# First eight heads reordered, early casts on ScalarE, and a shorter general path in an attention, expert and gated-layer kernel

## The chip, the cores and the metric

The kernel runs on one core of one Trainium2 chip. The metric is device microseconds of one execution, the median of the runs.

## The reference

```python
def _attn_ref(q, k, v, g_q, g_k):          # q, k, v: (4, 12, 448, 64)
    q_n, k_n = rmsnorm(q, g_q), rmsnorm(k, g_k)
    scores = 1 / sqrt(64) * q_n @ k_n.T
    attn = exp(scores - max(scores)); attn /= sum(attn) + 1e-9
    return attn @ v

def _moe_ref(x, expert_emb, tau, w1, w2):  # x: (1792, 768), 8 experts, hidden 1024
    logits = (x / |x|) @ (expert_emb / |expert_emb|).T / tau
    e = argmax(logits); g = softmax(logits)[e]
    return g * (relu(x @ w1[e]) @ w2[e])

def _moe2_ref(x, w_gate, w_val, w_out):    # hidden 1536
    return (sigmoid(x @ w_gate) * (x @ w_val)) @ w_out
```

All is float32. The three run one after the other on the same 1792 rows.

## The kernel before

The program has three stages. `attention` goes over 48 heads (4 batches of 12). The 448 rows of a head lie on 112 partitions, 4 rows (r = 0 to 3) on each. Two heads form a group g; two or four heads are loaded as a unit u. `experts` sorts the rows by expert into a table in HBM and multiplies each expert's window of rows with its weights. `glu` is the gated layer. TensorE (PE) multiplies in pairs of float32r products: each operand is cast into a high part, and the rest, a low part, is subtracted.

The path of a head n in `attention`: `squares` and `stats` make the reciprocal root mean squares of q and k (for unit 0 a chain of ten small steps on VectorE, `rsqrt`; for later units two on ACT and five on GpSimd, `pool_rsqrt`). `scale_k` scales k; `scale_q` scales q, but for group 0, whose q is not scaled: there the scale goes into the maxima and the exponentials. `high_q` and `low_q` make the parts of q, `high_v` and `low_v` those of v. `turn_k` and `turn_q` transpose on PE; `high_k`, `low_k` and `copy_q` bring the results to SBUF, with the gain vector `gsc`. Then for each r: `scores` (two matmuls of PE), `peaks` (VectorE takes the negated maximum, L326; for the two heads of group 0 it multiplies it with the scale, L328), `exps` (ACT, L337), `turn_p` (four transposes), `high_p`, `low_p`, `values`. `copy_o`, `outputs` and `weigh` finish the head.

The scores have two PSUM buffers (`pss`), so the scores of a row block wait for the exponential two before it. `squares` runs on ACT for the first part of groups 0 to 3, on GpSimd later; group 0's k is squared by VectorE. `copy` takes an engine number: 0 is ACT, 1 VectorE, 3 GpSimd; `early(g)` is true for groups 1 to 7.

The order is written out by hand. Every call is put into a list by `at(place, f, ...)`; `chain` puts the steps of a generator one after the other, and `steps_of` takes some steps at one place. Places count row blocks, four to a head; `PLACE` holds those of the steady state, `EARLY` and `EARLY_LOADS` those of groups 1 to 7, and numbers below zero the time before head 0. The list is sorted by place, and each engine runs its instructions in that order. The DMA loads of q, k and v go on SP's queue, one unit after the other (`load`, L176), and so do the two gain vectors (`gains_load`, L598) between unit 0's q and v.

At the end of attention `plan` (on VectorE) works out from the experts' counts where each window lies, and `most`, how far the fullest expert exceeds its window. Meanwhile PE multiplies the first rows of the first expert (`soon_hidden`, taken in steps of two matmuls by `steps_of` at four places; L851). `load_most` (L862) brings `most` into a register of every engine, and `experts` starts with a branch (L1138): only where `most` is above zero is `beyond` run, a general path for experts with more rows than their window. With these inputs it is jumped over. PE goes on with L855.

```python
        with tc.If(soon["most"] > 0):
            beyond(pools)
```

Of the kernel before, what the change touches and what calls it, by code (L numbers as in the profile page):

```python
# [21 lines left out]
def tile_attention_moe_glu(  # L22
# [29 lines left out]
    MORE = min(WIN)  # L52
# [74 lines left out]
    EARLY_LOADS = [-19.988, -7.521, -2.583, 3.821, 11.99]  # L127
    EARLY = [
# [9 lines left out]
    def attention(ctx2, rp, after):  # L138
# [30 lines left out]
        def load(u):  # L169
# [3 lines left out]
            for src, dst in ((k, qk[:, 1]), (q, qk[:, 0]), (v, vv)):  # L173
# [455 lines left out]
        for g in range(NGT):  # L629
# [1161 lines left out]
```

## Time and profile before

| | |
|---|---|
| runs (three), us | 1183.16, 1183.21, 1185.81; median 1183.21 |
| profiled execution, us | 1183.76 |
| its span on the core, us | 1182.1 |
| PE busy | 1139.1 us (96%) |
| PE weight loads busy | 1053.4 us (89%) |
| VectorE busy | 867.3 us (73%) |
| ScalarE busy | 574.3 us (49%) |
| GpSimd busy | 319.1 us (27%) |
| DMA | 154.54 MB, 131 GB/s |

The span is what the profile covers; the execution's own time is 1.66 us longer. Busy shares are averages over stages of very different kind, so they are read by stretch.

### The profile page before, as it was taken

What the parts mean: (1) busy time and instruction counts of PE and PEld (TensorE: products, weight loads), DVE (VectorE), ACT (ScalarE), POOL (GpSimd) and SP (SyncE); (2) the same over time, 40 slices, a digit from 0 to 9 for tenths busy, and PEclk for the clock granted to TensorE, in tenths of its full rate; (3) what the DMA queues carried; (4) which work ended last, traced back from release to release, by engine and by line L of the source; (5) the groups of instructions that cost most, each with busy time, mean ns of one, the idle gap of its engine ahead of it and who ended that gap; (6) DMA issues with size and microseconds to landing.
All of it is one profiled execution on the core that took longest, in us unless ns stands there. A gap on an engine that the chain in (4) does not pass through costs nothing.

```text
span 1182.1 us, 19579 instructions
## 1 busy us (share of the span) xinstructions
PE 1139.1 (96%) x7198; PEld 1053.4 (89%) x7199; DVE 867.3 (73%) x1650; ACT 574.3 (49%) x1285; POOL 319.1 (27%) x484
## 2 busy tenths in 40 slices
PE   4899999999999999999999999999999999999996
PEld 3688888787888999999999999999999999999996
DVE  7999898898884145566677887887888878346673
ACT  5788988998993143556665521221212121332220
POOL 5765778779752000000000000010000000021132
PEclk9999999999999999999999999999999999999998
DMA  5414823111063164666676233443444343932031
GB/s 120 111 37 114 254 56 95 47 48 49 27 206 113 55 209 139 206 194 212 213 221 189 89 111 130 147 160 112 151 139 134 120 142 99 352 119 98 21 134 53
DMA packets 97942, 154.54 MB, mean 131 GB/s; under 512 B 4891, under 2 KB 82459, under 8 KB 96947
## 3 DMA queue, kind: packets, MB, share of 16 engines
q1 hardware_dynamic: 91379, 125.70, 34.8%
q0 software_dynamic: 6432, 27.53, 6.2%
q8 instruction: 58, 0.95, 0.3%
q14 instruction: 41, 0.34, 0.1%
q10 hardware_dynamic: 32, 0.02, 0.0%
HBM read 117.84 MB, written 35.39 MB: 130 GB/s over the span
## 4 chain that ended last, share of the span: by engine, by line
PE 62%; issue 3%; POOL 1%; DMA 1%; POOLq 0%
PE psg L1125 42%; PE pso L1125 8%; PE psg L1129 5%; PE psg L855 2%; PE psg L1132 2%; POOL out_dram L754 1%; PE psg L851 1%; PE psw L1160 1%; DMA wout<-wod 1%; PE psw L822 0%; POOL dummy L761 0%; PE pso L1103 0%; POOLq L1787 0%; POOLq L754 0%
## 5 line engine op out<-in xcount | busy, mean ns | idle before, releaser
L1125 PE MATMUL psg<-xs,w 128*128 128x448 f32 x1728 | 351.3, 365 | 0.0
L1125 PEld LDWEIGHTS psg<-xs,w 128*128 128x128 f32 x1728 | 323.9, 188 | 27.1
L1435 POOL DMA_DIRECT2D wod<-so x42 | 22.9, 544 | 604.2 <-DVE hA L1577 349.9
L1125 PE MATMUL pso<-wout,hs 128*128 128x384 f32 x882 | 153.4, 335 | 0.4 <-DMA wout<-wod 0.4
L1125 PEld LDWEIGHTS pso<-wout,hs 128*128 128x128 f32 x882 | 152.9, 188 | 0.7 <-issue 0.7
L978 DVE TENSOR_TENSOR whl<-raw,whl 128x768 fp32r<-128x768 f32 (+1 forms) x98 | 105.1, 1073 | 60.1 <-ACT whl L974 59.9
L337 ACT ACTIVATE pn<-pss,nm 112x448 f32<-112x448 f32 x184 | 119.7, 651 | 28.2 <-DVE nm L326 26.5
L326 DVE TENSOR_REDUCE nm<-pss 112x1 f32<-112x448 f32 x192 | 118.4, 617 | 8.9 <-PE pss L319 8.6
L374 DVE TENSOR_TENSOR pl<-pst,ph 112x448 fp32r<-112x448 f32 x180 | 110.6, 614 | 17.3 <-ACT ph L361 16.0
L354 PEld LDWEIGHTS pst<-ident,pn 112*112 112x112 f32 x768 | 88.0, 134 | 25.6 <-DVE pl L374 5.7
L354 PE MATMUL pst<-ident,pn 112*112 112x112 f32 x768 | 106.3, 260 | 4.5 <-DVE pl L374 4.4
L361 ACT CAST ph<-pst 112x448 fp32r<-112x448 f32 x180 | 97.3, 541 | 11.0 <-PE pst L354 8.1
L388 PE MATMUL psv<-ph,vt 112*128 112x448 f32 x204 | 91.8, 460 | 0.0
L319 PE MATMUL pss<-kh,qt 128*112 128x448 f32 x192 | 79.3, 413 | 12.8 <-ACT pn L337 11.7
L974 ACT CAST whl<-raw 128x768 fp32r<-128x768 f32 (+1 forms) x98 | 90.7, 926 | 0.0
L1413 ACT CAST w<-cva 128x384 fp32r<-128x384 f32 x48 | 24.7, 515 | 109.2 <-DVE cva L1397 104.2
L1125 PE MATMUL psg<-hhl,whl 128*128 128x288 f32 (+3 forms) x576 | 75.1, 287 | 0.0
L319 PE MATMUL pss<-kl,qt 128*112 128x448 f32 x192 | 71.8, 374 | 0.0
L1125 PEld LDWEIGHTS psg<-hhl,whl 128*128 128x128 f32 x576 | 70.9, 189 | 0.1
L1125 PE MATMUL psg<-xhl,whl 128*128 128x288 f32 (+3 forms) x576 | 70.0, 283 | 0.0
L1125 PEld LDWEIGHTS psg<-xhl,whl 128*128 128x128 f32 x576 | 69.4, 188 | 0.0
L388 PE MATMUL psv<-pl,vt 112*128 112x448 f32 x180 | 65.6, 365 | 0.0
(287 smaller groups left out, 2003.6 us busy)
## 6 DMA issues: line engine op xcount, KB each, us to landing
raw<-in_moe_w_dram SPq DMA_DIRECT2D x28, 768.0 KB, 4.5
raw<-in_moe_w_dram SPq DMA_DIRECT2D x21, 1024.0 KB, 5.4
wod<-so POOLq DMA_DIRECT2D x42, 384.0 KB, 2.6
wout<-wod SPq DMA_DIRECT2D x7, 2304.0 KB, 9.6
raw<-in_moe_w_gate_dram SPq DMA_DIRECT2D x24, 384.0 KB, 3.3
raw<-in_moe_w_val_dram SPq DMA_DIRECT2D x24, 384.0 KB, 3.2
raw<-in_moe_w_out_dram SPq DMA_DIRECT2D x24, 384.0 KB, 3.1
xs<-zero SPq DMA_DIRECT2D x8, 960.0 KB, 7.2
```

The lines of the kernel that those rows point to most:

```text
L319: nc.tensor.matmul(ps[:P, :S], lhsT=qt[:, r * P : (r + 1) * P], rhs=kk, start=(i == 0), stop=(i == 1))
L326: nc.vector.tensor_reduce(out=nm, in_=sc[n, r][:P, :S], axis=AX.X, op=ALU.max, negate=True)
L337: nc.scalar.activation(out=pn[n][:, r], in_=sc.pop((n, r))[:P, :S], func=AF.Exp, bias=sc.pop((n, r, "m")), scale=scale(0, 0, n, 1)[:, r] i ...
L354: nc.tensor.transpose(ps[:P, r * P : (r + 1) * P], p[:, r, c * P : (c + 1) * P], ident[:P, :P])
L361: nc.scalar.copy(out=ph, in_=pt[n, c][0][:P, :S])
L374: nc.vector.tensor_tensor(out=pl, in0=ps[:P, :S], in1=ph.bitcast(F32), op=ALU.subtract)
L388: nc.tensor.matmul(ps[:, :S], lhsT=lhs, rhs=p, start=(c == 0 and i == 0), stop=(c == R - 1 and i == len(parts) - 1),)
L974: nc.scalar.copy(out=splits[p][:, 0, cs], in_=raws[p][:, cs])
L978: nc.vector.tensor_tensor(out=w[:, 1, cs], in0=raws[p][:, cs], in1=w.bitcast(F32)[:, 0, cs], op=ALU.subtract)
L1125: nc.tensor.matmul(ps, lhsT=lhs[:, a], rhs=rhs[:, b], start=first and i == 0, stop=last and i == 2)
L1129: nc.tensor.matmul(ps.rearrange("p (a n) -> p a n", n=n), lhsT=lhs[:, 0], rhs=rhs, start=first, stop=False)
L1413: nc.scalar.copy(out=hi, in_=af)
```

## The change

What it does:

- `load` brings q ahead of k in every unit; unit 1's load is moved up behind unit 0's; the gain vectors are loaded from ACT's queue.
- In group 0 the casts and differences of q come first, and ACT squares k too, after the cast of q. The squares of groups 1 to 3 are put at places of their own.
- `scale_k`, `turn_k`, `high_k` and `low_k` of head 1 move behind the first scores of head 0. Head 2's steps stand at places of their own (`SECOND`).
- The first maxima (heads 0 and 1) are multiplied with the scale by ACT, ahead of the exponential, in place of VectorE; the product has a tile of its own.
- For groups 1 to 7 the casts `high_q` and `high_v` go from VectorE to ACT.
- `constants` (GpSimd) and the experts' norm come later.
- `soon_hidden` takes 29 steps in place of 25 ahead of the load of `most`.
- `beyond` is written with windows of 128 rows in place of 192 and loops over the weights' columns.

```diff
-    MORE = min(WIN)
+    MORE = 128
...
-        sum_squares=17.264, choice=16.838, norms=22.659, ranks=26.111, gate_x=45.151, second=9.104,
-        constants=7.485, emb_norm=1.692, emb_step=0.342, emb_turn=10.124, guard=-0.094, first_v=-13.224,
+        sum_squares=17.264, choice=16.838, norms=22.659, ranks=26.111, gate_x=45.151, 
+        constants=20.3, emb_norm=3.5, emb_step=0.342, emb_turn=13.3, guard=-0.094, first_v=-13.224,
     )
+    SECOND = (5.0, 5.35, 5.585, 5.9, 6.25)
...
-    EARLY_LOADS = [-19.988, -7.521, -2.583, 3.821, 11.99]
+    EARLY_LOADS = [-19.988, -19.987, -2.583, 3.821, 11.99]
     EARLY = [
-        [-12.0, 0.85, 1.0, 0.9, 2.342, 0.398, 2.863, 1.588],
...
+        [-19.8705, 1.43, 1.51, 1.5, 3.45, 6.6, 3.47, 7.0],
...
-            for src, dst in ((k, qk[:, 1]), (q, qk[:, 0]), (v, vv)):
+            for src, dst in ((q, qk[:, 0]), (k, qk[:, 1]), (v, vv)):
...
-            if i == 0 and (g < 4 or ENG_SQ[g % NG]):
+            if g == 0 or i == 0 and (g < 4 or ENG_SQ[g % NG]):
                 nc.scalar.activation(out=sq[:, sl], in_=x, func=AF.Square)
...
-            copy(0 if g == 0 else 1 if early(g) else ENG_QS[g % NG], qs[:, :, 0], heads(nat[unit_of[g][0]][0][:, 0], g))
+            copy(0 if g <= 7 else 1 if early(g) else ENG_QS[g % NG], qs[:, :, 0], heads(nat[unit_of[g][0]][0][:, 0], g))
...
-            copy(0 if g == 0 else 1 if early(g) else ENG_VT[g % NG], vt[:, :, D : 2 * D], heads(nat[unit_of[g][0]][1], g))
+            copy(0 if g <= 7 else 1 if early(g) else ENG_VT[g % NG], vt[:, :, D : 2 * D], heads(nat[unit_of[g][0]][1], g))
...
             if n < G:
-                nc.vector.tensor_tensor(out=nm, in0=nm, in1=scale(0, 0, n, 1)[:, r], op=ALU.mult)
+                raw, nm = nm, sm.tile([P, 1], F32, tag="nms", name="nms", bufs=4)
+                sc[n, r, "raw"] = raw
...
+            if n < G:
+                nc.scalar.activation(
+                    out=sc[n, r, "m"], in_=sc.pop((n, r, "raw")), func=AF.Copy, scale=scale(0, 0, n, 1)[:, r]
+                )
...
-                nc.sync.dma_start(out=t, in_=src.unsqueeze(0).to_broadcast([2, D]))
+                nc.scalar.dma_start(out=t, in_=src.unsqueeze(0).to_broadcast([2, D]))
...
-                for place, n in ((-0.4, 2), (0.16, 9), (0.17, 25), (1.2, 99)):
+                for place, n in ((-0.4, 2), (0.16, 9), (0.17, 29), (1.2, 99)):
...
-                halves(w1, NC, xt, F // 2, to_hidden)
-                halves(w2, nfc, ht, DM // 2, to_rows)
+                for w, kc, x, y, func in ((w1, NC, xt, ht, AF.Relu), (w2, nfc, ht, yt, AF.Copy)):
+                    to = y.rearrange("p f n -> p (f n)")
+                    with tc.For_i(0, w.shape[2], 128) as col:
+                        wa = ov.tile([128, nfc, 128], F32, tag="ow", name="ow")
+                        part = w[bass.ds(ex, 1), :, bass.ds(col, 128)]
+                        nc.sync.dma_start(out=wa[:, 0:kc], in_=part.rearrange("o (c p) f -> p (o c) f", p=128))
+                        ps = gemm_ps()[:, :MORE]
+                        for c in range(kc):
+                            nc.tensor.matmul(ps, lhsT=wa[:, c], rhs=x[:, c], start=(c == 0), stop=(c == kc - 1))
+                        nc.scalar.activation(out=to[:, bass.ds(col, MORE)], in_=ps, func=func)
```

In these rows sq, qs, qt, kh, kl, vt, nm, nms are the tiles of the steps named above, st those of the reciprocal roots; a number behind a name is its buffer. The beginning of ACT's program, before:

```order
L191 ACTIVATE sq_143<-qk_121 112x512
L267 CAST qs_145<-qk_121 112x8x64
L267 CAST qt_153<-psq_148 128x448
L287 ACTIVATE kh_171<-psk_165,gsc_71 128x448
L267 CAST qt_178<-psq_173 128x448
L287 ACTIVATE kh_185<-psk_180,gsc_71 128x448
L267 CAST vt0_116<-vv_122 112x8x64
L191 ACTIVATE sq_207<-qk_135 112x1024
```

and now:

```order
L604 DMA gsc_71<-in_g_q_dram 128x1x1
L604 DMA gk_125<-in_g_k_dram 128x1x1
L268 CAST qs_129<-qk_121 112x8x64
L192 ACTIVATE sq_135<-qk_121 112x512
L192 ACTIVATE sq_138<-qk_121 112x512
L268 CAST qt_158<-psq_153 128x448
L192 ACTIVATE sq_163<-qk_140 112x1024
L288 ACTIVATE kh_180<-psk_174,gsc_71 128x448
L268 CAST qt_187<-psq_182 128x448
L268 CAST vt0_116<-vv_122 112x8x64
```

The gain vectors' loads stand first, the cast of q ahead of both squares, and a square of unit 1 (112x1024) ahead of the first `high_k`. The second `high_k` is gone from here. PE at the same place, before:

```order
L301 MATMUL psq_148<-ident_70,qs_145 128x112 x4
L281 MATMUL psk_165<-ident_70,ks_162 128x112 x4
L301 MATMUL psq_173<-ident_70,qs_145 128x112 x4
L281 MATMUL psk_180<-ident_70,ks_162 128x112 x4
L319 MATMUL pss_229<-kh_171,qt_153 112x448
L319 MATMUL pss_229<-kl_191,qt_153 112x448
L319 MATMUL pss_240<-kh_171,qt_153 112x448
L319 MATMUL pss_240<-kl_191,qt_153 112x448
```

and now:

```order
L302 MATMUL psq_153<-ident_70,qs_129 128x112 x4
L282 MATMUL psk_174<-ident_70,ks_172 128x112 x4
L302 MATMUL psq_182<-ident_70,qs_129 128x112 x4
L320 MATMUL pss_218<-kh_180,qt_158 112x448
L320 MATMUL pss_218<-kl_200,qt_158 112x448
L320 MATMUL pss_229<-kh_180,qt_158 112x448
L320 MATMUL pss_229<-kl_200,qt_158 112x448
L282 MATMUL psk_238<-ident_70,ks_172 128x112 x4
```

The transposes of head 1's k (the second psk) stand behind the first two pairs of scores. VectorE, up to its first maximum (nm), before:

```order
L73 TENSOR_SCALAR st0_129<-st1_130 112x8
L292 SCALAR_TENSOR_TENSOR kl_191<-psk_165,gsc_71,kh_171 128x448
L78 TENSOR_TENSOR st1_130<-st0_129 112x8
L80 TENSOR_TENSOR st1_130<-st1_130,st2_131 112x8
L82 SCALAR_TENSOR_TENSOR st1_130<-st1_130 112x8
L84 SCALAR_TENSOR_TENSOR st0_129<-st1_130,st0_129 112x8
L86 TENSOR_TENSOR st1_130<-st0_129 112x8
L88 SCALAR_TENSOR_TENSOR st1_130<-st1_130,st2_131 112x8
L292 SCALAR_TENSOR_TENSOR kl_199<-psk_180,gsc_71,kh_185 128x448
L90 SCALAR_TENSOR_TENSOR st0_129<-st1_130,st0_129 112x8
L326 TENSOR_REDUCE nm_232<-pss_229 112x1
L328 TENSOR_TENSOR nm_232<-nm_232,st0_129 112x1
```

and now:

```order
L73 TENSOR_SCALAR st0_132<-st1_133 112x8
L78 TENSOR_TENSOR st1_133<-st0_132 112x8
L293 SCALAR_TENSOR_TENSOR kl_200<-psk_174,gsc_71,kh_180 128x448
L80 TENSOR_TENSOR st1_133<-st1_133,st2_134 112x8
L82 SCALAR_TENSOR_TENSOR st1_133<-st1_133 112x8
L84 SCALAR_TENSOR_TENSOR st0_132<-st1_133,st0_132 112x8
L86 TENSOR_TENSOR st1_133<-st0_132 112x8
L88 SCALAR_TENSOR_TENSOR st1_133<-st1_133,st2_134 112x8
L90 SCALAR_TENSOR_TENSOR st0_132<-st1_133,st0_132 112x8
L327 TENSOR_REDUCE nm_222<-pss_218 112x1
L327 TENSOR_REDUCE nm_232<-pss_229 112x1
L234 TENSOR_TENSOR ks_172<-qk_121,st0_132 112x512
```

The second `low_k` (kl) and the product L328 are gone, and half of the scaling of k (ks) comes behind two maxima. PE at the branch around `beyond`, before (oxw, oxt, oht and ow are the tiles of `beyond`):

```order
L1138 COMPARE_AND_BRANCH
L1325 COMPARE_AND_BRANCH
L1325 UNCONDITIONAL_BRANCH x2
L1787 BRANCH_PREFETCH_HINT
L1326 ISA
L1326 TENSOR_LOAD tabs
L1326 COMPARE_AND_BRANCH
L1336 MATMUL psg<-ident,oxw 128x96 x12
L1350 MATMUL psg<-oxt,ow 128x192 x48
L1350 MATMUL psg<-oht,ow 128x192 x48
```

and now:

```order
L1150 COMPARE_AND_BRANCH
L1336 COMPARE_AND_BRANCH
L1336 UNCONDITIONAL_BRANCH x2
L1784 BRANCH_PREFETCH_HINT
L1337 ISA
L1337 TENSOR_LOAD tabs
L1337 COMPARE_AND_BRANCH
L1348 MATMUL psg<-ident,oxw 128x128 x6
L1352 COMPARE_AND_BRANCH
L1352 UNCONDITIONAL_BRANCH x2
L1784 BRANCH_PREFETCH_HINT
L1358 MATMUL psg<-oxt,ow 128x128 x6
```

Between the branch and the end of `beyond` there were 12, 48 and 48 matmuls; there are 6 and 6 here and 8 in a second loop behind these rows.

## Rows read from the trace of the kernel before

**Rows 1.** windows: us, busy us (instructions) by engine, PE to POOL; clock, DMA

```profile
15.94:33.95 18.01, 12.26 (x55) 9.03 (x56) 15.89 (x30) 12.44 (x32) 14.51 (x38) 1.00 0.38 90
33.95:50.00 16.05, 13.40 (x97) 10.65 (x95) 15.86 (x29) 11.67 (x32) 9.44 (x14) 1.00 0.37 88
50.00:80.00 30.00, 28.83 (x201) 24.03 (x202) 27.69 (x52) 25.83 (x69) 21.59 (x26) 1.00 0.20 47
80.00:116.00 36.00, 35.26 (x252) 29.35 (x251) 34.18 (x67) 30.81 (x82) 18.65 (x19) 1.00 0.44 120
```

**Rows 2.** timeline, first 16 us: start, us, engine, line, operation, tiles [idle before]

```profile
4.04 0.69 DVE L193 TENSOR_TENSOR sq<-qk 112x512 f32<-112x512 f32 x1 [3.92 <-DMA qk<-in_k_dram]
...
4.57 0.63 ACT L191 ACTIVATE sq<-qk 112x512 f32<-112x512 f32 x1 [2.44 <-DMA qk<-in_q_dram]
...
5.10 0.60 ACT L267 CAST qs<-qk 112x512 fp32r<-112x512 f32 x1
...
5.70 0.17 DVE L69 TENSOR_SCALAR st<-st 112x8 int32<-112x8 int32 x1
5.78 1.26 POOL L251 TENSOR_TENSOR qs<-qk,qs 112x512 fp32r<-112x512 f32 x1 [2.48 <-ACT qs L267]
5.90 1.16 DVE L73 TENSOR_SCALAR st<-st 112x8 int32<-112x8 int32 x1
...
8.50 1.29 DVE L233 TENSOR_TENSOR ks<-qk,st 112x512 f32<-112x512 f32 x2
...
11.63 1.01 PE L281 MATMUL psk<-ident,ks 112*128 112x112 f32 x4 [0.62 <-ACT qt L267]
...
13.94 1.24 DVE L90 SCALAR_TENSOR_TENSOR st<-st,st 112x8 f32<-112x8 f32 x1
...
15.94 0.72 ACT L337 ACTIVATE pn<-pss,nm,st 112x448 f32<-112x448 f32 x1 [0.23 <-DVE nm L328]
```

**Rows 3.** DMA view, 2 to 8 us: busy tenths and GB/s in 40 slices

```profile
DMA  9437999999752000099499999000000000003799
GB/s 150 109 109 273 355 328 396 362 348 205 171 116 48 0 0 0 0 41 75 41 130 151 89 68 21 0 0 0 0 0 0 0 0 1 0 21 137 253 328 328
```

**Rows 4.** timeline: a cast and a one-element operation on ACT

```profile
13.20 0.61 ACT L267 CAST vt<-vv 112x512 fp32r<-112x512 f32 x1
...
24.61 0.18 ACT L96 ACTIVATE en<-en 8x1 f32<-8x1 f32 x1
```

**Rows 5.** lines view, DVE, 0 to 34 us: count, busy us, mean ns

```profile
L328 DVE TENSOR_TENSOR nm<-nm,st 112x1 f32<-112x1 f32 x8 | 3.4, 430 | 0.3
```

**Rows 6.** windows view of line L271 alone: us, DVE busy us (instructions)

```profile
33.95:116.00 82.05, 7.77 (x11) 1.00 0.34 87
```

**Rows 7.** timeline, 366 to 391 us, PE around the branch

```profile
366.89 7.04 PE L851 MATMUL psg<-soon_x,soon_w 128*128 128x160 f32 x50
...
374.38 3.50 PE L851 MATMUL psg<-soon_x,soon_w 128*128 128x160 f32 x24 [0.45 <-issue]
...
380.17 10.61 PE L855 MATMUL psg<-soon_hh,soon_w 128*128 128x160 f32 x64 [2.29 <-PEq L1138]
```

**Rows 8.** line L1138 by sequencer: ns min, median, max; start us

```profile
L1138 DVEq COMPARE_BRANCH  x1: 72/72/72, 374.4 to 374.4; - x1
...
L1138 PEldq COMPARE_BRANCH  x1: 4406/4406/4406, 375.3 to 375.3; - x1
L1138 POOLq COMPARE_BRANCH  x1: 45/45/45, 376.0 to 376.0; - x1
```

**Rows 9.** view of line L862: the register load on PE

```profile
L862 PEldq TENSOR_LOAD <-most x1: 1178/1178/1178, 373.1 to 373.1; - x1
```

**Rows 10.** windows view, 380 to 388 us, columns as in rows 1

```profile
380.20:382.00 1.80, 1.80 (x9) 1.80 (x10) 0.00 (x0) 0.00 (x0) 0.25 (x2) 0.64 0.31 57
382.00:384.00 2.00, 2.00 (x9) 2.00 (x9) 0.00 (x0) 0.00 (x0) 0.00 (x0) 0.50 0.77 229
...
386.00:388.00 2.00, 2.00 (x17) 2.00 (x16) 0.00 (x0) 0.00 (x0) 0.00 (x0) 1.00 0.32 119
```

More of the change, by code (lines that the diff above doesn't have):

```diff
@@ L636, in attention @@
             if g:
-                chain(ts, 0.2 if g > 1 else 0.8, squares(g, later=14))
+                if g < 4:
+                    work = squares(g)
+                    for place in (ts, *((0.925, 0.93), (2.95, 2.96), (9.4, 9.6))[g - 1]):
+                        at(place, steps_of, work, 1)
+                else:
+                    chain(ts, 0.2, squares(g, later=14))
                 if j == 0:
@@ L645, in attention @@
         at(start, load, 0)
-        chain(start, 0.001, squares(0, 1, 1))
-        chain(start + 0.125, 0, squares(0, 0, 1), 1, start + 0.21)
+        at(start + 0.001, high_q, 0)
+        at(start + 0.002, low_q, 0)
+        chain(start + 0.003, 0.001, squares(0, 1, 1))
+        chain(start + 0.005, 0, squares(0, 0, 1), 1, start + 0.21)
         chain(start + 0.1, 0.01, stats(0, 1, 1))
@@ L651, in attention @@
         for place, f, *a in (
-            (0.126, high_q, 0), (0.127, low_q, 0), (0.202, scale_k, 0, 0, 1), (0.203, scale_k, 0, 1, 1),
-            (0.128, turn_q, 0), (0.129, copy_q, 0), (0.206, turn_q, 1), (0.207, copy_q, 1),
-            (0.204, turn_k, 0), (0.205, high_k, 0), (0.2225, low_k, 0),
-            (0.208, turn_k, 1), (0.209, high_k, 1), (0.2285, low_k, 1),
+            (0.128, turn_q, 0), (0.129, copy_q, 0), (0.202, scale_k, 0, 0, 1),
+            (0.204, turn_k, 0), (0.205, high_k, 0), (0.206, turn_q, 1), (0.207, copy_q, 1), (0.2235, low_k, 0),
         ):
             at(start + place, f, *a)
-        at(PLACE["first_v"], high_v, 0)
-        at(PLACE["first_v"], low_v, 0)
+        at(-19.7908, high_v, 0)
+        at(-0.09, low_v, 0)
+        for place, f, *a in ((0.922, scale_k, 0, 1, 1), (0.93, turn_k, 1), (1.42, high_k, 1), (1.95, low_k, 1)):
+            at(place, f, *a)
         for n in range(N):
-            lead = {0: -8.5, G: PLACE["second"]}.get(n, n * R)
-            for f in (turn_k, high_k, low_k, turn_q, copy_q) if n >= G else ():
-                at(lead + PLACE[f.__name__], f, n)
+            for i, f in enumerate((turn_k, high_k, low_k, turn_q, copy_q) if n >= G else ()):
+                at(SECOND[i] if n == G else n * R + PLACE[f.__name__], f, n)
             for r in range(R):
@@ L1296, in beyond @@
     def beyond(pools):
[L1298 removed]
+        K = -(-(NT - min(WIN)) // MORE)
         N = E * K
[L1300 removed]
         ov = tc.alloc_tile_pool(name="ov", bufs=1, side="left")
@@ L1340, in beyond @@
-                ht = ov.tile([128, nfc, MORE], F32, tag="oht", name="oht")
-                def halves(w, kc, x, width, evict):
-                    for h in range(2):
-                        wa = ov.tile([128, kc, width], F32, tag="ow", name="ow")
-                        part = w[bass.ds(ex, 1), :, h * width : (h + 1) * width]
-                        nc.sync.dma_start(out=wa, in_=part.rearrange("o (c p) f -> p (o c) f", p=128))
-                        for f in range(width // 128):
-                            ps = gemm_ps()
-                            for c in range(kc):
-                                nc.tensor.matmul(
-                                    ps[:, :MORE], lhsT=wa[:, c, f * 128 : (f + 1) * 128], rhs=x[:, c],
-                                    start=(c == 0), stop=(c == kc - 1),
-                                )
-                            evict(h * width // 128 + f, ps[:, :MORE])
@@ L1356, in to_hidden @@
-                def to_hidden(f, ps):
-                    nc.scalar.activation(out=ht[:, f], in_=ps, func=AF.Relu)
-                def to_rows(o, ps):
-                    nc.scalar.copy(out=x2[:, o, bass.ds(dst, MORE)], in_=ps)
-                halves(w1, NC, xt, F // 2, to_hidden)
-                halves(w2, nfc, ht, DM // 2, to_rows)
+                xw = ov.tile([MORE, DM], F32, name="oxw")
+                nc.sync.dma_start(out=xw, in_=xs[bass.ds(src, MORE)])
+                xt, ht, yt = [ov.tile([128, n, MORE], F32, name=name) for name, n in (("oxt", NC), ("oht", nfc), ("oyt", NC))]
@@ new lines, in beyond @@
+                for c0 in range(0, NC, 4):
+                    n = min(4, NC - c0)
+                    ps = gemm_ps()[:, : n * MORE].rearrange("p (c n) -> p c n", n=MORE)
+                    for c in range(n):
+                        nc.tensor.transpose(ps[:, c], xw[:, (c0 + c) * 128 : (c0 + c + 1) * 128], ident)
+                    nc.scalar.copy(out=xt[:, c0 : c0 + n], in_=ps)
+                for w, kc, x, y, func in ((w1, NC, xt, ht, AF.Relu), (w2, nfc, ht, yt, AF.Copy)):
[8 more added lines that the diff above has]
+                        nc.scalar.activation(out=to[:, bass.ds(col, MORE)], in_=ps, func=func)
@@ L1364, in beyond @@
+                nc.scalar.copy(out=x2[:, :, bass.ds(dst, MORE)], in_=yt)
         ov.release()
```

12 lines of the change are left out of this document (removed), and 4 rows, old and new, of the table EARLY.

## The prediction

> **What bounds the kernel now.** I read the busy tenths first: PE stands at 9 in all but the first and the last slices, so time can only be won where PE stands idle or runs slowly. The windows view gives those places. From the first exponential at 15.94 us to the ninth, at 33.95 us, PE is busy 12.26 of 18.01 us; then it idles 2.65, 1.17 and 0.74 us in the three stretches to 116 us [rows 1]. The reader is to see there that VectorE (DVE) is busy 15.86 of 16.05 us after 33.95 us while ScalarE (ACT) has 4.38 us free. The timeline of the first 16 us shows why the first exponential is so late [rows 2], and a second look, at 366 to 391 us, shows the one later place where PE stops: the branch around `beyond` [rows 7]. From there to the output layer PE does not wait, so what is won before stays won.
>
> **The change part by part.** I split it in four terms.
>
> *A, until the first exponential.* Before, k landed at 4.04 us and q at 4.57 us; VectorE squared k (0.69), its 0.17 us chain of reciprocal-root steps began, and one step took 1.16 us because it started 0.12 us after GpSimd (POOL) had begun the 1.26 us `low_q` [rows 2]. Now q lands first, ACT casts it at once (0.60), GpSimd subtracts at about 4.7 to 6.0 us, and ACT squares k at about 4.6 to 5.2 us (0.63, the row of its square of q). VectorE starts reducing 0.5 us later than before but with GpSimd done: 1.16 becomes 0.17. So k's scaling, at 8.50 before, begins at about 8.0. It is now half the work (1.29 for two instructions), and the second head's transposes, which stood ahead of the scores at 11.63 for 1.01 us, stand behind two pairs of scores. VectorE loses one `low_k` ahead of the first maximum. Counting from 8.0: half a scaling 0.65, the small product 0.15 (taken as one 0.17 step), a reduction 0.69 (as the square), ten steps of 0.2 with their gaps, one `low_k` of about 0.7, make 12.2; the stall of the last step (1.24 for 0.17) may stay, as `low_v` still comes then: 12.2 to 13.3. A maximum (0.6) and the new one-element product on ACT (0.18, the one-element operation [rows 4]) put the first exponential at 13.0 to 14.1. Against that stand two waits: ACT now squares unit 1 ahead of `high_k`, so it waits for unit 1's q and k there, and the gain vectors move from SP's queue, behind q and k, to ACT's, beside them. Their tiny pieces kept the DMA engines busy for 8 slices of 0.15 us, 1.2 us [rows 3]; if k came that much later, 0.6 to 1.7 us of the gain would be left, and a wait for unit 1's loads can take the rest. Bounds: 0 to 2.9 us won; I take 1.4, the middle, since both waits are possible and neither is in the trace. Swapping q and k in the later units' loads costs nothing, as those come long before their use; if they did not, it would be one load's 0.5 us, the step from 4.04 to 4.57.
>
> *B, the first eight exponentials.* ACT was busy 12.44 of these 18.01 us [rows 1]. It gets eight one-element products (8 x 0.18 to 0.2 = 1.6 us), three casts at 0.61 [rows 4] = 1.8, and one `high_k` that used to lie ahead (about 0.6): 16.4 us of work. VectorE is rid of the eight products, 3.4 us [rows 5]. So ACT takes over as the bound and the stretch cannot get under 16.4; with 0.6 us of hand-overs 17.0. Won: 1.0. Bounds: 1.6 won if ACT never waits, 1.5 lost if each product and exponential waits for its maximum as often as before.
>
> *C, 33.95 to 116 us.* Eleven casts leave VectorE, 7.77 us [rows 6], and cost ACT 11 x 0.61 = 6.7. VectorE was the fullest engine in the first of the stretches, and ACT had 16.05 - 11.67 + 30.00 - 25.83 + 36.00 - 30.81 = 13.7 us free, so they fit. PE idled 4.56 us there; I take back a quarter, 1.2, since part of it is waiting for ACT, which gets fuller. Bounds: 4.5 won; 1.5 lost, about a quarter of ACT's new 6.7. Moving `constants` and the expert norms costs nothing: their readers come after the first twelve heads; if that cover failed it would be their operations of some 0.2 us, once.
>
> *D, the branch.* Each engine loads `most` and jumps over `beyond`. On PE the load took 1.178 us from 373.1 [rows 9]; its 50 matmuls ended at 373.93 and the next began at 374.38, an idle 0.45 us [rows 7]. Eight more matmuls now stand ahead of the load (29 steps for 25), 8 x 0.146 = 1.17 us of work, so this gap closes: 0.45. Then the branch took PE's sequencer 4.406 us, and the other engines' 0.045 to 0.072 us [rows 8]; the 24 queued matmuls ran out at 377.88 and PE began again at 380.17, 2.29 us idle. [...] What differs on PE is the length of the jump: 108 listed matmuls before, 20 now, while GpSimd's and VectorE's regions hold none. If the short jump costs what theirs cost, the 16 matmuls left after the load cover it, PE never stops, and 0.45 + 2.29 + 1.65 = 4.4 us are won. If it costs 4.406 as before, eight fewer matmuls follow the load, so the branch starts and PE resumes only about 0.3 us earlier. I take 4.4, as the new jump lies nearer to the short rows.
>
> [...]
>
> Sum: 1.4 + 1.0 + 1.2 + 4.4 = 8.0 us. The profiled execution took 1183.76 us, so 1175.8 there; the median of the runs is 0.55 lower, so I say 1175.2.
>
> **The rivals.** *The branch still waits.* The price may come from leaving the region at all and not from its length; for it: only one PE branch is in the trace; against it: four other engines left in under 0.1 us. Then 1183.2 - 3.6 - 0.3 = 1179.3.
>
> *The start gives nothing.* The gain vectors' pieces get between q and k (1.2 us), ACT waits for unit 1's loads ahead of `high_k`, and A and B come to zero with C: 1183.2 - 4.4 = 1178.8. For it: 1.2 us of busy DMA engines [rows 3]; against it: ACT issues them after its table load, SP its q and k at once. [...]
>
> *Slower: ACT becomes the bound.* The mechanism is in C: an exponential waits for a cast ahead of it, the scores' two buffers stay full, and PE waits. It decides once ACT's free 13.7 us are gone in the stretches where PE needs them. All 6.7 us of new casts on the path, nothing from A and B, and the branch still waiting: 1183.2 + 6.7 - 0.3 = 1189.6. Against it: ACT is at 73 to 86% there.
>
> **How the numbers follow.** 0.3%, 3.5 us, is about what a measurement can tell from no change. Forecast 0.70 (its own spread 1172 to 1178, nearly all faster); branch still waits 0.15 (about three in five faster, as 3.9 us lies just past the line); the start gives nothing 0.11 (nearly all faster); ACT bound 0.04. So faster is 0.87, same 0.09, slower 0.04. The low end takes A, B and C at 2.4, 1.6 and 3.3 with D: 11.7 us, 1171.5; the high end takes in both middle rivals and a little more, 1180.0.
>
> **What would show it.** Right: a first exponential at 13 to 15 us, the ninth at 30 to 32.5, PE's branch row under 0.2 us, no idle on PE around it, a granted clock of 1.00 in the 4 us behind it. A wrong: the first square of k on ACT begins after 6 us. B and C wrong: ACT over 95% busy from 34 to 116 us, with PE waiting for exponentials. D wrong: a branch of microseconds on PE again; it is more than half of the sum, so this decides most.

## The result and the profile after

| | before | now |
|---|---|---|
| runs beside each other, us | 1185.81 median of 5 (1183.16 to 1186.48) | 1173.16 median of 5 (1172.93 to 1174.91) |
| profiled execution, us | 1183.76 | 1173.17 |
| its span, us | 1182.1 | 1171.5 |

The ratio is 0.9901, 95% interval 0.9887 to 0.9914: faster by about 11.7 us by this ratio (12.65 between the medians), and by 10.6 us between the two profiled executions. 1175.2 us was forecast. The kernel before had medians of 1184.85, 1184.03 and 1184.76 us in the three later sets of runs, 10.9 to 11.7 us above the changed kernel's, so the gain is known to one or two microseconds. Below, the stages are read from the profiled executions, where every start is known, and the medians are set beside them.

The page of the kernel now, its line of busy time and three lines of the slices:

```profile
PE 1134.6 (97%) x7198; PEld 1051.6 (90%) x7199; DVE 853.7 (73%) x1627; ACT 582.8 (50%) x1308; POOL 318.8 (27%) x484
...
PE   5999999998999999999999999999999999999996
...
DVE  5899888898884165566677878877898878336663
ACT  7999998998983144565566522121212122332220
```

The reader is to see that PE stands at 9 in all slices but the first, the tenth and the last, and that ScalarE (ACT) stands at 8 or 9 from the second slice to the twelfth, where VectorE (DVE) does too: the two share the early work.

The stages are marked by exponentials, counted in order of their starts (the first, 9th, 60th and last of 192), and by VectorE's first copy into `late` (L1209 before, L1221 now), which follows PE's products behind the branch.

| stage, us | before | now | won | forecast |
|---|---|---|---|---|
| A, to the first exponential | 15.94 | 15.59 | 0.35 | 1.4 |
| B, to the 9th | 18.01 | 16.38 | 1.63 | 1.0 |
| C, to the 60th | 91.82 | 88.14 | 3.68 | 1.2 |
| to the last | 227.34 | 227.35 | 0.0 | 0 |
| D, to the first copy into `late` | 38.91 | 34.71 | 4.20 | 4.4 |
| to the end | 790.06 | 789.32 | 0.74 | 0 |
| sum | 1182.08 | 1171.49 | 10.59 | 8.0 |

C's forecast was worked out for 33.95 to 116 us; PE's idle time is nearly the same to the 60th exponential, 4.57 us against 4.56, so the two are set side by side. The starts behind the table are 15.94, 33.95, 125.77, 353.11 and 392.02 us before, and 15.59, 31.97, 120.11, 347.46 and 382.17 us now.

Timeline of the kernel now, 3 to 16 us, which answers to [rows 2]:

```profile
3.74 0.62 ACT L268 CAST qs<-qk 112x512 fp32r<-112x512 f32 x1 [1.60 <-DMA qk<-in_q_dram]
...
4.99 1.15 ACT L192 ACTIVATE sq<-qk 112x512 f32<-112x512 f32 x2 [0.64 <-DMA qk<-in_k_dram]
...
8.39 0.69 DVE L234 TENSOR_TENSOR ks<-qk,st 112x512 f32<-112x512 f32 x1
...
9.14 1.01 PE L282 MATMUL psk<-ident,ks 112*128 112x112 f32 x4 [2.38 <-DVE ks L234]
...
10.19 1.06 ACT L192 ACTIVATE sq<-qk 112x1024 f32<-112x1024 f32 x1 [2.86 <-DMA qk<-in_k_dram]
...
11.15 0.62 ACT L288 ACTIVATE kh<-psk,gsc 128x448 fp32r<-128x448 f32 x1
...
11.80 0.68 DVE L293 SCALAR_TENSOR_TENSOR kl<-psk,gsc,kh 128x448 fp32r<-128x448 f32 x1 [0.97 <-ACT kh L288]
...
12.79 1.28 POOL L261 TENSOR_TENSOR vt<-vv,vt 112x512 fp32r<-112x512 f32 x1 [7.09 <-ACT vt L268]
12.79 1.30 DVE L84 SCALAR_TENSOR_TENSOR st<-st,st 112x8 f32<-112x8 f32 x1
...
15.26 0.29 ACT L340 ACTIVATE nms<-nm,st 112x1 f32<-112x1 f32 x1 [1.59 <-DVE nm L327]
15.59 0.72 ACT L343 ACTIVATE pn<-pss,nms,st 112x448 f32<-112x448 f32 x1
```

q is cast at 3.74 us, as forecast. But ACT's square of unit 1 waits 2.86 us for that unit's k, until 10.19; the first `high_k` (kh) stands behind it at 11.15, though its transposes (9.14) were done at 10.15, a microsecond earlier; VectorE's `low_k` (kl) waits 0.97 us for it. Then one step of the chain takes 1.30 us instead of 0.17, beside GpSimd's `low_v`, which began at the same 12.79.

One profile does not size A. In five profiles of kernels with this same start (now, and the branch experiments below) the first exponential lies at 15.14 to 16.00 us; in three with the old start (before, and two more below) at 15.70 to 16.05.

Windows view, columns as in [rows 1], of B and C now:

```profile
15.59:31.97 16.38, 12.21 (x62) 8.93 (x62) 10.79 (x19) 15.97 (x43) 12.41 (x22) 1.00 0.50 127
...
31.97:120.11 88.14, 85.47 (x621) 73.12 (x619) 81.04 (x153) 81.98 (x214) 58.78 (x83) 1.00 0.37 104
```

And C in the kernel before:

```profile
33.95:125.77 91.82, 87.25 (x622) 72.96 (x621) 87.04 (x162) 77.16 (x203) 57.02 (x67) 1.00 0.38 103
```

In C, VectorE did 6.0 us less and ACT 4.8 us more, and the stretch became 3.7 us shorter. What ACT waited for there, by the view of waits (us in total, times, longest), before and now:

```profile
ACT pn L337 <- DVE nm L326: 13.0, 20, 1.6
```

```profile
ACT pn L343 <- DVE nm L327: 4.5, 13, 1.1
```

ACT's exponentials waited 13.0 us for VectorE's maxima, and now wait 4.5.

Timeline of PE around the branch now, its rows L1150 by sequencer, and the windows behind it. They answer to [rows 7, 8, 10]:

```profile
361.25 10.30 PE L863 MATMUL psg<-soon_x,soon_w 128*128 128x160 f32 x74
...
372.00 8.93 PE L867 MATMUL psg<-soon_hh,soon_w 128*128 128x160 f32 x64 [0.45 <-PEq L1150]
```

```profile
L1150 PEldq EVENT_SEMAPHORE  x2: 51/51/51, 371.6 to 371.7; - x2
...
L1150 PEldq COMPARE_BRANCH  x1: 363/363/363, 369.0 to 369.0; - x1
```

```profile
371.00:373.00 2.00, 1.55 (x12) 1.34 (x11) 0.00 (x0) 0.44 (x1) 0.50 (x4) 1.00 0.80 241
373.00:375.00 2.00, 2.00 (x17) 2.00 (x16) 0.00 (x0) 0.00 (x0) 0.00 (x0) 1.00 0.11 43
```

The branch takes 0.363 us where it took 4.406. PE is idle for 0.45 us before its next product, and the granted clock stays at 1.00.

### The profile page after: what moved, and what is told of

It is laid out like the page before. It is cut to its first block, busy times and chain, and to the rows that moved or that the text cites. A ratio compares the mean times of both kernels' runs of the same rounds, so it can differ in the third digit from the quotient of the medians.

```text
span 1171.5 us, 19563 instructions
## 1 busy us (share of the span) xinstructions
PE 1134.6 (97%) x7198; PEld 1051.6 (90%) x7199; DVE 853.7 (73%) x1627; ACT 582.8 (50%) x1308; POOL 318.8 (27%) x484
## 4 chain that ended last, share of the span: by engine, by line
PE 63%; issue 3%; POOL 1%; POOLq 0%
PE psg L1137 42%; PE pso L1137 9%; PE psg L1141 5%; PE psg L1144 2%; PE psg L867 2%; POOL out_dram L766 1%; PE psg L863 1%; PE psw L1172 1%; PE psw L834 0%; POOL dummy L773 0%; PE pso L1115 0%; POOLq L1784 0%; POOLq L766 0%
```

## The experiments

Diffs are against the changed kernel, but for two runs that start from the kernel before, as said there. Ratios are to the kernel before, run beside each.

### The branch: the old general path in the changed kernel

```diff
-    MORE = 128
+    MORE = min(WIN)
...
-                for w, kc, x, y, func in ((w1, NC, xt, ht, AF.Relu), (w2, nfc, ht, yt, AF.Copy)):
...
+                halves(w1, NC, xt, F // 2, to_hidden)
+                halves(w2, nfc, ht, DM // 2, to_rows)
```

> The changed kernel with the general path of before. Theory (the length of PE's jump sets the price of the branch): PE's branch row is microseconds again, near 4.4 us, PE stands idle over 2 us behind the load of the flag, the granted clock falls after it, and the span is 4.0 to 4.4 us above the changed kernel's 1171.5. Rival (the gain there came from the four more steps ahead of the load, or from the earlier start): the branch row stays under 0.5 us and the span within 0.7 us of 1171.5.

1176.58 us (4 runs, 1175.48 to 1177.34), ratio 0.9933 (0.9917 to 0.9950). PE around the branch, and the branch:

```profile
361.59 10.30 PE L863 MATMUL psg<-soon_x,soon_w 128*128 128x160 f32 x74
...
373.42 8.93 PE L867 MATMUL psg<-soon_hh,soon_w 128*128 128x160 f32 x64 [1.53 <-PEq L1150]
```

```profile
L1150 PEldq COMPARE_BRANCH  x1: 3646/3646/3646, 369.3 to 369.3; - x1
```

The branch is back at 3.646 us, so the general path does set its price. But in this profile D is 35.78 us, only 1.07 more than with the short path, where theory and rival expected about 4 us and under 0.7 for the span; the span is 2.3 us longer. Of the 4.2 us of D, 3.13 are kept without the short path: the gap at the load stays closed (0.45), PE is idle for 1.53 us and not 2.29, and no half clock (the 0.50 of [rows 10]) follows: the 64 matmuls behind the branch take 8.93 us, as in the changed kernel, and not 10.61 [rows 7]. The 0.76 us of idle time are the branch itself, which is shorter by 4.406 - 3.646 = 0.76. It also began sooner, 0.2 us after the end of the load (367.9 + 1.182, then 369.3) where it had been 1.0 (373.1 + 1.178, then 375.3 [rows 8, 9]); but the matmuls behind the load are fewer and ran out that much sooner too. The forecast's other price for D, 0.3 us if the branch still waits, kept both the branch's time and the half clock as they were, and neither stayed in this profile. By the medians the old path costs more, 3.4 us: the profiled execution was the fastest of the four, and the other spans are 1.0 to 1.9 us longer at mean granted clocks of 0.994 to 0.996 against 0.997. No profile shows where they lost it; a half clock behind the branch is possible, so the 1.07 us of one profile may be too little.

### The branch: 25 steps ahead of the load again

```diff
-                for place, n in ((-0.4, 2), (0.16, 9), (0.17, 29), (1.2, 99)):
+                for place, n in ((-0.4, 2), (0.16, 9), (0.17, 25), (1.2, 99)):
```

> The changed kernel with 25 steps of the hidden product ahead of the load of the flag, as before. Theory (the eight matmuls only close the gap at the load): PE idles some 0.45 us at the load and the span grows by 0.3 to 0.5 us; what stands behind the branch is unchanged. Rival (the steps no longer matter, since the branch is short): span within 0.2 us.

1173.61 us (one run); the branch 0.358 us, D 35.40 us: 0.69 more than with 29 steps. PE is idle twice for 0.45 us, at the load and at the branch, as in the rows of the next run. So four steps more close the gap at the load, as said. The one median is only 0.45 us above the changed kernel's, within the spread of its runs.

### The branch: the kernel before with the short path alone

Against the kernel before:

```diff
-    MORE = min(WIN)
+    MORE = 128
...
-                halves(w1, NC, xt, F // 2, to_hidden)
-                halves(w2, nfc, ht, DM // 2, to_rows)
+                for w, kc, x, y, func in ((w1, NC, xt, ht, AF.Relu), (w2, nfc, ht, yt, AF.Copy)):
...
```

> The kernel before with only the short general path (25 steps stay). Theory (the long jump's branch ran PE out of matmuls, and the slow clock came after that): the branch row on PE falls from 4.41 to about 0.36 us, 0.45 us idle at the load and about 0.45 at the branch are left, no clock fall; from the last exponential to the first `late` copy 38.9 becomes 35.4, and the median is 3.5 us below the kernel before. Rival (the changed kernel with the old path lost only 1.07 us in this stage, so the path is worth about that wherever it stands, and the rest of the stage came from elsewhere in the change): 37.8 us for the stage, median about 1.1 us below.

1182.25 us (11 runs, 1179.92 to 1184.14) against 1184.76 (21 runs), ratio 0.9976 (0.9966 to 0.9987), which is 2.8 us (1.5 to 4.0). PE around the branch, and the branch:

```profile
368.55 7.04 PE L851 MATMUL psg<-soon_x,soon_w 128*128 128x160 f32 x50
...
376.05 3.50 PE L851 MATMUL psg<-soon_x,soon_w 128*128 128x160 f32 x24 [0.46 <-issue]
...
380.00 8.93 PE L855 MATMUL psg<-soon_hh,soon_w 128*128 128x160 f32 x64 [0.45 <-PEq L1138]
```

```profile
L1138 PEldq COMPARE_BRANCH  x1: 358/358/358, 377.0 to 377.0; - x1
```

D is 35.42 us, 3.49 less than before, and no half clock follows. The theory holds, and its rival falls, whose 1.1 us lie outside the interval too: PE's idle time at the branch goes from 2.29 to 0.45 us, which is 1.84, and the other 1.65 us are what the prediction gave for the half clock that does not come. By the profiles the two parts of D overlap: the short path alone wins 3.49 us, the changed kernel without it 38.91 - 35.78 = 3.13, both together 4.20. In these two profiles PE was idle for at most 1.53 us in one piece at the branch, and no half clock followed. The medians do not show the overlap: the path is worth 2.8 us alone (2.5 between the medians) and 3.4 in the changed kernel. The ratio shows 0.7 us less than the stage, within its interval; 0.35 of it lie outside the span, since each of these eleven executions stands 2.0 us above its span, where those of the kernel before stand 1.7. This profile lost time elsewhere: PE was busy for 1.38 of 2.60 us, and then the granted clock was 0.50 from 37.6 to 44.4 us:

```profile
35.00:37.60 2.60, 1.38 (x14) 1.06 (x13) 2.60 (x5) 1.01 (x4) 0.00 (x0) 1.00 0.05 13
37.60:44.40 6.80, 6.80 (x32) 6.04 (x32) 4.45 (x10) 4.69 (x14) 6.24 (x9) 0.50 0.53 134
```

### The branch: how its price grows with the region's length

24 matmuls (and, in a second run, 72), whose result is not used, at the end of the general path, which is jumped over:

```diff
+                ps = gemm_ps()[:, :MORE]
+                for c in range(24):
+                    nc.tensor.matmul(ps, lhsT=ht[:, c % nfc], rhs=ht[:, 0], start=(c == 0), stop=(c == 24 - 1))
+                nc.scalar.activation(out=oz, in_=ps, func=AF.Copy)
```

> The changed kernel with 24 more matmuls in the general path, which is not run: some 100 more PE instructions to jump over (44 listed matmuls in place of 20). Theory A (the price follows the length, step by step): PE's branch row grows by about a quarter to a third of the way from 0.36 to 4.4 us, to 1.4 us or so. Theory B (there is a point up to which a jump is short): still 0.3 to 0.5 us and the same span within 0.3 us.

> The changed kernel with 72 more matmuls in the general path, which is not run: 92 listed matmuls to jump over, about as much PE program as before the change. Theory (length alone): PE's branch row is back near 4.4 us, with over 2 us of idle PE and a lower clock behind it, span about 4 us above 1171.5. Rival (the form of the old path mattered, straight code in place of loops): the branch stays under 0.5 us and the span the same.

The branch with 24, which makes 44 listed matmuls in the region:

```profile
L1150 PEldq COMPARE_BRANCH  x1: 357/357/357, 372.1 to 372.1; - x1
```

And with 72, which makes 92:

```profile
L1150 PEldq COMPARE_BRANCH  x1: 3526/3526/3526, 370.8 to 370.8; - x1
```

With 20, 44, 92 and 108 matmuls the changed kernel's branch takes 0.363, 0.357, 3.526 and 3.646 us. By these single profiles the price is a step between 44 and 92, not a price per matmul. D is 34.85 and 35.74 us in these two runs. Their times, 1177.70 and 1177.02 us (one run each), are above the changed kernel's mostly elsewhere: the stage to the last exponential is 3.2 and 1.5 us longer, as the last section shows, and the stretch to the end 1.3 and 0.9.

What PE waits for in a branch of 3.5 us is in no profile here, and what sets the place of the step was not tried apart.

### The casts: back on VectorE in the changed kernel

```diff
-            copy(0 if g <= 7 else 1 if early(g) else ENG_QS[g % NG], qs[:, :, 0], heads(nat[unit_of[g][0]][0][:, 0], g))
+            copy(0 if g == 0 else 1 if early(g) else ENG_QS[g % NG], qs[:, :, 0], heads(nat[unit_of[g][0]][0][:, 0], g))
...
-            copy(0 if g <= 7 else 1 if early(g) else ENG_VT[g % NG], vt[:, :, D : 2 * D], heads(nat[unit_of[g][0]][1], g))
+            copy(0 if g == 0 else 1 if early(g) else ENG_VT[g % NG], vt[:, :, D : 2 * D], heads(nat[unit_of[g][0]][1], g))
```

> The changed kernel with the fourteen casts of groups 1 to 7 back on VectorE. Theory (the casts make most of what was won from the ninth exponential to 126 us, 3.7 us): the first exponential stays at 15.6 us, the sixtieth comes 2.5 to 4 us later than 120.1, span 1174 to 1175.5. Rival (the order of steps and the later constants won it, the casts only changed sides): span within 1 us of 1171.5.

1179.18 us (4 runs, 1178.24 to 1180.07), ratio 0.9955 (0.9938 to 0.9972): 6.0 us more than the changed kernel's median. C is back at 91.97 us (32.35 to 124.32), 3.83 more, and ACT again waits for the maxima:

```profile
ACT pn L343 <- DVE nm L327: 11.0, 18, 1.6
```

B is longer too, by 0.77 us, though ACT has three casts less to do there (columns as in [rows 1]):

```profile
15.20:32.35 17.15, 14.07 (x62) 10.78 (x62) 13.18 (x22) 14.74 (x41) 12.77 (x22) 1.00 0.50 121
```

The theory holds for C. Its span, 1174 to 1175.5 us, was missed: 1177.3. Besides C and B, 0.83 us lie in the stage to the last exponential, where the granted clock was 0.50 from 295.1 to 298.5 us, and in the median 0.35 us lie outside the span, 2.0 us in place of 1.7 in each run.

### The casts: the kernel before with the casts on ScalarE alone

The same two lines, the other way round, in the kernel before.

> The kernel before with only the fourteen casts of groups 1 to 7 moved from VectorE to ScalarE. Theory (the casts make all of term C by themselves): first exponential as before, about 15.9 us; from the ninth to the 60th 91.8 becomes 88.1 us, the last exponential is 4 to 5 us earlier, the median 4 to 5.5 us below the kernel before. Rival (the casts pay only since the first heads' other work was spread differently, squares and products included): 90.5 us or more for that stretch and at most 1.5 us in the median.

1180.63 us (11 runs, 1179.34 to 1184.65) against 1184.76 (21 runs), ratio 0.9969 (0.9959 to 0.9980), which is 3.7 us (2.4 to 4.9). C is 88.33 us (33.27 to 121.60), so 3.49 of the 3.68 us of C are the casts alone; B is 17.22 us, 0.80 less than before, also by them. The windows view of C, and what ACT waits for there:

```profile
33.27:121.60 88.33, 85.46 (x624) 73.62 (x622) 81.07 (x151) 82.03 (x213) 56.33 (x67) 1.00 0.38 105
```

```profile
ACT pn L337 <- DVE nm L326: 5.4, 14, 1.1
```

VectorE is busy 6 us less than before, ACT 4.9 more, and ACT's wait for the maxima falls from 13.0 to 5.4. The branch waits as before (4.586 us, and the half clock behind it). The theory holds; the last exponential is 3.96 us earlier, where 4 to 5 was expected, and the medians differ by 4.1 us.

### The start: unit 1's square behind the first `high_k`

```diff
-        [-19.8705, 1.43, 1.51, 1.5, 3.45, 6.6, 3.47, 7.0],
+        [-19.7945, 1.43, 1.51, 1.5, 3.45, 6.6, 3.47, 7.0],
```

> The changed kernel with the square of unit 1 behind the first high part of k on ACT. Theory (that square waits for unit 1's loads until 10.19 us and holds the high part up from 10.2 to 11.15): the first exponential comes 0.7 to 1.0 us earlier, at 14.6 to 14.9, and the span is 0.3 to 1.0 us shorter. Rival (the first maximum waits for VectorE's root chain and its stall behind GpSimd, not for the scores): the first exponential stays at 15.3 to 15.7 and the span the same.

1172.68 us (4 runs, 1172.05 to 1174.05), ratio 0.9904 (0.9887 to 0.9920). The start:

```profile
9.53 1.01 PE L282 MATMUL psk<-ident,ks 112*128 112x112 f32 x4 [2.72 <-DVE ks L234]
...
10.58 0.63 ACT L288 ACTIVATE kh<-psk,gsc 128x448 fp32r<-128x448 f32 x1 [3.20 <-PE psk L282]
...
11.11 1.04 ACT L192 ACTIVATE sq<-qk 112x1024 f32<-112x1024 f32 x1
11.25 0.68 DVE L293 SCALAR_TENSOR_TENSOR kl<-psk,gsc,kh 128x448 fp32r<-128x448 f32 x1 [0.19 <-ACT kh L288]
...
12.24 0.17 DVE L84 SCALAR_TENSOR_TENSOR st<-st,st 112x8 f32<-112x8 f32 x1
...
12.93 1.18 DVE L327 TENSOR_REDUCE nm<-pss 112x1 f32<-112x448 f32 x2
...
14.27 0.72 ACT L343 ACTIVATE pn<-pss,nms,st 112x448 f32<-112x448 f32 x1
```

`high_k` begins at once behind its transposes, `low_k` at 11.25, and the chain's step takes its 0.17 us again, since `low_v` now begins when the chain is over (13.18). The first exponential is at 14.27 us, 1.32 earlier than now, the 9th at 30.65, also 1.32 earlier, where 0.7 to 1.0 was expected, and the span is 1170.7, 0.8 less. So the square's wait is what A failed on. In the medians the two are not told apart: 0.5 us, with intervals that overlap nearly wholly.

### The start: both squares of unit 1 later

```diff
-        [-19.8705, 1.43, 1.51, 1.5, 3.45, 6.6, 3.47, 7.0],
-        [-19.7905, 5.201, 7.354, 6.499, 8.935, 1.907, 10.142, 4.65],
+        [-19.7945, 1.43, 1.51, 1.5, 3.45, 6.6, 3.47, 7.0],
+        [0.12, 5.201, 7.354, 6.499, 8.935, 1.907, 10.142, 4.65],
```

> The changed kernel with both squares of unit 1 later on ScalarE: group 1's behind the first high_k, as in the run with the square later, and group 2's behind the expert-embedding loads, just ahead of the first exponential's product. Theory (what ScalarE does ahead of the first product sets the first exponential): first exponential at 13.9 to 14.3 us, within 0.3 us of the 14.27 with one square moved, and the span 0.8 to 1.1 us below the changed kernel's 1171.5. Rival (the square is only pushed on to a place where VectorE's sums wait for it): first exponential as early, but the 60th at 119.5 us or later, and no gain in the median (1173.2).

1172.49 us (4 runs, 1171.90 to 1173.99), ratio 0.9894 (0.9879 to 0.9909). The first exponential is at 14.21 us and the 60th at 118.80, so the rival's late 60th exponential is not there, but the second square stayed ahead of the first product and won nothing more. The profiled span, 1172.3, is not lower as expected: PE waited 1.3 us in the gated layer (last section). The spans of the other three executions are 1170.2 to 1170.9. This is the lowest median of the study, and not told apart from the changed kernel's.

### The start: the gain vectors on SP's queue again

```diff
-                nc.scalar.dma_start(out=t, in_=src.unsqueeze(0).to_broadcast([2, D]))
+                nc.sync.dma_start(out=t, in_=src.unsqueeze(0).to_broadcast([2, D]))
```

> The changed kernel with the gain vectors back on SP's queue between q, k and v of unit 0. Theory (on ACT's queue they lie beside k, which came at 4.99 in place of 4.57): k is squared at 4.4 to 4.7 us, but v and unit 1 come later by 1 to 3 us, so ACT waits longer at unit 1's square and the first exponential comes 0.5 to 2.5 us later; span 0.3 to 2.5 us longer. Rival (the queue does not matter): first exponential within 0.3 us of 15.59, span the same.

1173.86 us (4 runs, 1173.51 to 1175.48), ratio 0.9915 (0.9899 to 0.9932). The first exponential is at 15.41 us, where the changed kernel's is at 15.59, and over the runs here with the same start it lies anywhere from 15.14 to 16.00; the 0.5 to 2.5 us later of the theory did not come. ACT's squares at the start, first those of unit 0's k and q, then that of unit 1:

```profile
4.65 1.14 ACT L192 ACTIVATE sq<-qk 112x512 f32<-112x512 f32 x2
...
10.01 1.06 ACT L192 ACTIVATE sq<-qk 112x1024 f32<-112x1024 f32 x1 [2.28 <-DMA qk<-in_k_dram]
```

ACT squares k at 4.65 us, as the theory said, without waiting for it; with the vectors on ACT's queue it waits, and starts at 4.72 to 5.34 in the five profiles with that start. So k may land some tenths of a microsecond later beside the vectors, while q is cast earlier there (3.64 to 3.92 us, 4.12 here). But `high_k` still stands behind the square of unit 1, at 10.97 us, so the earlier k cannot show in the first exponential. The queue costs nothing while that square waits; what it would cost with the square moved was not tried. So the rival that the start gives nothing has these few tenths of k for it, and in the time no run here shows them.

### The first heads: the product with the scale on VectorE again

```diff
-                raw, nm = nm, sm.tile([P, 1], F32, tag="nms", name="nms", bufs=4)
-                sc[n, r, "raw"] = raw
+                nc.vector.tensor_tensor(out=nm, in0=nm, in1=scale(0, 0, n, 1)[:, r], op=ALU.mult)
...
-            if n < G:
-                nc.scalar.activation(
-                    out=sc[n, r, "m"], in_=sc.pop((n, r, "raw")), func=AF.Copy, scale=scale(0, 0, n, 1)[:, r]
-                )
```

> The changed kernel with the eight one-element products back on VectorE. Theory (ACT is the bound of the first eight exponentials, so the product there costs about what it saves on VectorE): the ninth exponential within 0.7 us of 31.97, span within 0.7 us of 1171.5. Rival (VectorE's products, 0.43 us each, held the exponentials up): ninth exponential 1 to 2.5 us later, and the span too.

1174.01 us (4 runs, 1173.67 to 1174.41), ratio 0.9912 (0.9895 to 0.9929). The first exponential is at 15.63 us and the 9th at 32.41, so B takes 16.78 us, 0.40 more than now; the span is 0.9 longer, a little over the 0.7 of the theory and under the 1 us of the rival. ACT has less to do in B and again waits for VectorE, where the changed kernel's view of waits has no such row (one of its two waits is that ahead of the first exponential):

```profile
15.63:32.41 16.78, 13.17 (x62) 10.36 (x62) 12.99 (x26) 14.21 (x36) 12.10 (x22) 1.00 0.47 124
```

```profile
ACT pn L338 <- DVE nm L329: 2.9, 2, 1.8
```

So ACT alone does not bound B: with 1.76 us less of work for it the stretch is longer.

## Why the prediction was right, by its steps

The time, 1173.16 us, lies in the range, and the side is right. Between the profiled executions the sum is 2.6 us short, and three of the four terms were not of the size given. That the time still came within 2.0 us is partly luck: A was 1.05 too high while B and C were 3.1 too low together.

**A, too high: 0.35 for 1.4.** The step that failed is "12.2 to 13.3" for the end of VectorE's chain; it ended at 14.7. k's scaling began at 8.39, not 8.0, as k landed 0.4 us later than q had before. VectorE waited 0.97 us for `high_k`, which waited behind the square for unit 1's load. That wait was named, as one of two that could take the gain; the middle between none and both was taken, and it came nearly in full. The run with the square later gives 1.32 us back, so it was this wait that decided. The other profiles agree: in the five with the same start, in the run with the casts back and in that with the gain vectors on SP's queue, unit 1's square starts at 9.75 to 10.60 us, and the first exponential comes 5.39 to 5.40 us behind it each time. The other wait, on the gain vectors, is hidden behind this one. The ground that ACT issues them behind its table load did not hold: the issue began at 0.89 us, the table load ran from 0.85 to 2.13. The sign named for a wrong A, a first square of k after 6 us, did not come (it began at 4.99), so it looked at the wrong wait; the first exponential at 15.59 is past the 13 to 15 us named as right.

**B, right in ACT's work, not in what else bounds: 1.63 for 1.0.** ACT is nearly full, as said: busy 15.97 of 16.38 us. The 0.6 us kept for hand-overs were nearly not needed; the stretch came down to the 16.4 that were worked out as ACT's work. Its product, in seven places 2.04 us, costs ACT less than the 3.4 us that VectorE is rid of, and moving it is worth 0.40. But the three casts, which the sum counted only as work for ACT, win 0.77 (0.80 in the kernel before): taking work off ACT made the stretch longer in both runs, as VectorE got it back and ACT waited for its maxima. The other 0.4 to 0.5 us of B, with the new order of the steps, were not tried alone.

**C, mis-sized: 3.68 for 1.2.** "I take back a quarter" of PE's idle 4.56 us was the failed step, in two ways. First, ACT's free 13.7 us were taken as room that costs when filled. The prediction left out the view of its waits, which says that most of its idle time ahead of exponentials was a wait for VectorE's maxima (13.0 us of the stretch to the 60th). Relieving VectorE shortened what ACT waits for (13.0 to 4.5 us), so both engines gained, and the fear that part of the idle time would become a wait for ACT had little ground. Second, PE's idle time as the windows give it was not the ceiling. To the 60th exponential PE's idle time fell from 4.57 to 2.67 us, and its busy time from 87.25 to 85.47 with the same matmuls (622 and 621 records): the mean length of each kind of matmul is the same within 2 ns, and all lengths add up to 188.8 and 188.7 us. So the records overlapped less in the stretch that took longer, and the PE that was idle for 1.9 us more was also busy for 1.8 more.

**D, right: 4.20 for 4.4.** The gap at the load closed, the branch's idle time went from 2.29 to 0.45 us, and the clock stayed at 1.00. No run shows the 1.65 us given for the half clock as such: they were an estimate from the clocks of [rows 10]. What the runs show in its place is the 64 matmuls behind the branch, 10.61 us before [rows 7] and 8.93 now, 1.68 less. Two details were off, and both were signs named for a right forecast. PE's branch takes 0.36 us, not under 0.2 as the other engines' 0.045 to 0.072. And PE is still idle at the branch, 0.45 to 0.73 us in all nine profiles with a branch of 0.36 us: here PE's two semaphore instructions of that line stand at 371.6 and 371.7 us, when the matmuls ahead, done at 371.55, are out of the way, long after the branch itself (369.0 us). The alternative of 0.3 us was wrong, as the first run shows; the rival "the branch still waits" would have given about 1176.6 us and not 1179.3, as the run with the old path does (its A, B and C were sized too low as well).

**Not in the sum: 0.74 us behind D.** PE waited once, 0.4 us, for a weight load in the gated layer before; now it does not wait there. Other runs have this wait with other lengths, so it is not counted to the change. The other 0.3 us were not traced.

The rival on the other side, ACT as the bound, needed ACT's free time to run out: it has 81.98 us of work in 88.14, and PE waits for exponentials no more than before (2.2 us in place of 2.3).

## What to carry to other kernels

Before calling an engine's idle time room, read what it waits for: idle time spent waiting for the fuller engine can shrink when work moves over from there, as ACT's wait for the maxima did here, from 13.0 to 4.5 us. A branch on PE over a region that is never run had a price by the region's length here, in a step (0.36 us over 20 and 44 listed matmuls, 3.5 to 4.6 over 92 and 108); shorten the region, and queue enough work ahead of the register load that PE does not run dry there (0.69 us of the stage here). When work is moved forward in an engine's program, look at the load that it waits for: one square ahead of its data gave back 1.32 of the 1.67 us that reordering the start had won (15.94 us before, 14.27 without that wait, 15.59 with it, one profile each).

## What the runs showed of the hardware that was not expected

**Half clock in other places.** The two runs with padding lost time far from the branch, each to two stretches of half clock (from 202.6 and 291.3 us with 24 matmuls, from 203.1 and 291.8 with 72). In the run with 72, PE's timeline from 201 us, and the windows around 203.1 us:

```profile
201.31 0.59 PE L360 MATMUL pst<-ident,pn 112*112 112x112 f32 x4 [1.25 <-DVE pl L380]
...
202.59 0.46 PE L320 MATMUL pss<-kh,qt 128*112 128x448 f32 x1 [0.28 <-ACT pn L343]
```

```profile
195.00:203.10 8.10, 6.58 (x47) 5.39 (x46) 5.80 (x11) 4.87 (x14) 7.86 (x8) 1.00 0.34 94
203.10:206.50 3.40, 3.40 (x16) 3.05 (x15) 2.69 (x7) 2.92 (x9) 2.84 (x7) 0.50 0.00 0
```

PE was idle for 1.25 and 0.28 us, and then the granted clock stood at 0.50 until 206.5 us. But the waits do not decide it: the changed kernel has the same two there, 1.29 and 0.28 us, and no less idle time around them, without a fall:

```profile
195.00:203.10 8.10, 6.53 (x47) 5.35 (x46) 5.65 (x12) 4.87 (x13) 7.79 (x8) 1.00 0.29 82
```

The padding lies behind the attention and is jumped over, so that it should cause this is not to be expected; but both padded kernels, run once each, have their falls at these places, and of the other profiles only that with the casts back on VectorE has one near them (295.1 us). This stays open. That runs of one kernel differ in the clock is shown: the eleven runs of the kernel before with the short path went from 1179.9 us at a mean granted clock of 0.998 to 1184.1 at 0.991. A single profile counts or misses such a fall. The old path in the changed kernel left PE idle for 1.53 us in one piece without one, so idle time alone does not say when it comes.

**A wait far behind the change.** PE's waits from 400 us on, before and in the run with both squares later:

```profile
PE pso L1125 <- DMA wout<-wod: 0.4, 1, 0.4
```

```profile
PE pso L1137 <- DMA wout<-wod: 1.3, 1, 1.3
```

The changed kernel's profile has no such row. Where a weight load of the gated layer lands against PE varied by up to 1.3 us between runs, more than the last experiments differ by.

**The long branch has two times.** With 24 matmuls behind the load it took 4.406 and 4.586 us (the kernel before, and the casts alone), with 16 behind it 3.646 and 3.526 us (the old path, and 72 matmuls of padding). What the 0.9 us between them are was not tried.
